# Score tiles of the second batch inside the first softmax chain of a cross-covariance attention and highway kernel, with five copies moved to ScalarE

## Chip, cores, metric

One core of a Trainium2 chip. The time is device microseconds (us) of a whole execution, the median of several; executions of the kernel before agree within about 0.3% here. A ratio is the mean time of one kernel's runs over that of the other's of the same rounds, so it is not quite the ratio of the medians quoted.

## The reference, cut

```python
# q, k, v: (B=4, N=6336, C=256), float32; tau = 1
qn = q / (norm(q, axis=1, keepdims=True) + 1e-6)
kn = k / (norm(k, axis=1, keepdims=True) + 1e-6)
s = kn.transpose(0, 2, 1) @ qn / tau            # (B, C, C): the scores
a = exp(s - s.max(-1)); a /= a.sum(-1) + 1e-9
x = (v @ a).reshape(B * N, C)
H = maximum(x @ w_h, 0); T = sigmoid(x @ w_t + b_t)
out = T * H + (1 - T) * x
```

The scores of a batch need all its rows of q and k; only then can its softmax be taken, and only then the first of its outputs.

## The kernel before

The loads of q and k come in groups of 3 to 8 tiles (a "k group" below). TensorE sums the scores of a batch over 49 tiles of 128 rows and a rest of 64: per tile `S` (k times q, two products of 256 columns) and the squares for the norms in `G` (four products of 128 columns, or two where ScalarE takes the squares of q). A **chain** turns them into matrices: norms, inverse, scaling, exponential, transposition, products with the weights, scaled copies. The outputs come in 100 **slots** of two tiles each: the gate product into a `zbank`, products `h` and `x`, and the transposition of a later pair of v tiles. The score tiles of batches 1 to 3 are mixed into the slots of the batch ahead. Only the first chain has no slots to lie beside; there TensorE multiplied zeros to keep its clock up: with them the granted clock was 1.00 from 37.1 to 45.2, and in a_old_loads, where TensorE stood idle from about 38.0 to 41.0, it fell to 0.50. All instructions stand in the order that the program writes them.

```python
    WARM = (14, 9)             # zero products in the two gaps of the first chain
    CHAIN0 = (0, 0, 0, 4)      # score tiles of batch 1 at four places of it
    PE_BIAS = (8, 67, 75, 97)  # slots whose gate gets its bias by two products; elsewhere ScalarE copies it
# ... at the start of the third group of batch 0:
            load_v(0)
            load_w()
            load_q(QFIRST[1])
            load_k(QFIRST[1])
            load_v(1)
# ... the first chain:
    c0["norms"]()
    c0["invs"]()
    keep_warm(WARM[0])
    fill(CHAIN0[0])
    c0["cq"]()
    c0["logits"]()
    turns = [(t, transpose(t)) for t in range(2)]
    fill(CHAIN0[1])
    keep_warm(WARM[1])
    c0["exps"]()
    c0["at"]()
    fill(CHAIN0[2])
    c0["at_copy"]()
    c0["softmax"]()
    vt_copy(*turns[0])
    c0["first_ahats"]()        # products with the weights, then scaled copies into mr
    vt_copy(*turns[1])
    fill(CHAIN0[3])
    for t in range(2, LOOK):   # LOOK = 3: pair 2
        vt_copy(t, transpose(t))
# ... in first_ahats, its end:
            ah = hx_tile("ah0_0")
            for ic in range(2):
                ahat_half(ah, 0, ic, False)
            for ic in range(2):
                scaled_copy(ah, 0, ic, ic == 0)      # half 0 by ScalarE, half 1 by VectorE
# ... one slot t (cut):
        for s in zs:
            mains(s, zbank[s % 2], 2, True)
            gate_act(s, zbank[s % 2])
        for s in by_pe[:1]:
            vt_copy(s, transpose(s))                 # pair t + 3
        for s in zs:
            seed(s, zbank[s % 2])
        mains(t, h, 1, False)
        mains(t, x, 0, False)
```

All transposed pairs pass through one PSUM bank, `vt_bank`, in two halves by turns.

Of the kernel before, what the change touches and what calls it, by code (L numbers as in the profile page):

```python
# [19 lines left out]
def kernel(  # L20
# [19 lines left out]
    nc = tc.nc  # L40
# [10 lines left out]
    def spans(*sizes):  # L51
        got, s0 = [], 0
        for ns in sizes:
            got.append((s0, ns))
            s0 += ns
        assert s0 == NS
        return got

    QG = [spans(8, 8, 8, 8, 8, 6, 3), spans(4, 8, 8, 8, 8, 8, 5)]
    QG += [spans(5, 8, 8, 8, 8, 8, 4)] * (B - 2)  # L60
    QALL = [(b, g) for b in range(B) for g in range(len(QG[b]))]
    QFIRST = [QALL.index((b, 0)) for b in range(B)]
    QTILES = 8
    QRING = 4
    ORING = 8
    DEFER = 6
    DRAIN = [59, 67, 64, 92, 72, 82]
    VG = [spans(6, 10, 12, 12, 9)] + [spans(12, 12, 12, 13)] * (B - 1)
    VTILES = 13
    VALL = [(b, g) for b in range(B) for g in range(len(VG[b]))]  # L70
# [1 line left out]
    VRING = 4  # L72
    NPAIR = (NS + 1) // 2
    LOOK = 3
    RAMP = 15
    REM_SLOT = 2
    START_US = 1

    WARM = (14, 9)

    CHAIN0 = (0, 0, 0, 4)
    HEAD = sum(CHAIN0)
    P1_END = [18, 42, 63]

    GATES = {14: 2, 19: 2, 20: 0, 22: 0, 25: 2, 27: 2, 33: 0, 54: 2, 55: 1, 60: 2, 66: 0, 68: 0, 70: 0, 95: 2}
    TURNS = {46: 2, 47: 2, 55: 2, 65: 0, 67: 0, 79: 0, 93: 2}
    VTS = 9
    OLAST = 2
    TTS = 6

    TGROUPS = ((26, 6, 73), (38, 6, 79))

    PE_BIAS = (8, 67, 75, 97)

    DVE_SUBS = (98, 99)

# [2 lines left out]



    SQ_RUNS = {1: (5, 20, 30), 2: (8, 18, 26, 35), 3: (10, 21, 34)}
    SQ_TILES = 8
    SQ_CUTS = 4
    SQ_RATE = 2
    LULL = [2, 3, 0, 5]

    EARLY = {"sums": (0, "pre"), "norms": (0, "pre"), "invs": (1, "pre"), "cq": (1, "pe"), "logits": (2, "pre"), "exps": (2, "post"), "softmax": (5, "pre"), "at": (5, "pe"), "at_copy": (6, "pre"), "ahat": (6, "pe"), "ahat_copy": (7, "pre")}
    MID = {"sums": (0, "pre"), "norms": (0, "pre"), "invs": (2, "pre"), "cq": (2, "pe"), "logits": (2, "post"), "exps": (3, "post"), "softmax": (3, "post"), "at": (5, "pe"), "at_copy": (6, "pre"), "ahat": (6, "pe"), "ahat_copy": (7, "pre")}
    LAST = {"sums": (0, "pre"), "norms": (0, "pre"), "invs": (1, "pre"), "cq": (2, "pe"), "logits": (2, "post"), "exps": (3, "pre"), "softmax": (7, "pre"), "at": (8, "pe"), "at_copy": (9, "pre"), "ahat": (9, "pe"), "ahat_copy": (10, "pre")}  # L110
    PLACES = [None, EARLY, MID, LAST]

    ctx.enter_context(tc.manual_schedule())
# [7 lines left out]
    def rows(src2d):  # L121
        return src2d[0:NF, :].rearrange("(p s) c -> p s c", s=NS)
# [4 lines left out]
    def load_q(n):  # L127
        b, g = QALL[n]
        s0, ns = QG[b][g]
        q_t[n] = stream_pool.tile([P, QTILES, C], f16, tag="q_in", bufs=QRING, name=f"q{n}")  # L130
        nc.gpsimd.dma_start(out=q_t[n][:, 0:ns, :], in_=rows(q[b])[:, s0 : s0 + ns, :])  # L131

    def load_k(n):
        b, g = QALL[n]
        s0, ns = QG[b][g]
        k_t[n] = stream_pool.tile([P, QTILES, C], f16, tag="k_in", bufs=QRING, name=f"k{n}")
        nc.gpsimd.dma_start(out=k_t[n][:, 0:ns, :], in_=rows(k[b])[:, s0 : s0 + ns, :])

    def load_v(m):
        b, g = VALL[m]  # L140
        s0, ns = VG[b][g]
        v_t[m] = stream_pool.tile([P, VTILES, C], f16, tag="v_in", bufs=VRING, name=f"v{m}")
        nc.gpsimd.dma_start(out=v_t[m][:, 0:ns, :], in_=rows(v[b])[:, s0 : s0 + ns, :])
# [99 lines left out]
    def squared(b, j):  # L243

        for n, j0 in enumerate(SQ_RUNS.get(b, ())):
            count = SQ_TILES - (n > 0)
# [10 lines left out]
    def squares(b, j):  # L257
# [24 lines left out]
        add_up(len(cuts))  # L282
        more = n < len(SQ_RUNS[b]) - 1
        if more:
# [12 lines left out]
    def add_up(k):  # L297
        while k > 0 and cuts:
            dst, source = cuts.pop(0)
            nc.vector.tensor_reduce(  # L300
                out=dst, in_=source, op=AluOp.add, axis=mybir.AxisListType.XY
            )
            k -= 1
# [225 lines left out]
    def v_of(b, s):  # L529
        if s == NS:  # L530
            return rem_t["v"][:, b, :]
        g = max(i for i in range(len(VG[b])) if VG[b][i][0] <= s)
        return v_t[VFIRST[b] + g][:, s - VG[b][g][0], :]
# [4 lines left out]
    def dma_transposes(t):  # L538

        for n, (s0, ns, at) in enumerate(TGROUPS):  # L540
            if at != t:
# [16 lines left out]

    for s0, ns, _ in TGROUPS:
        for i in range(s0 // 2, (s0 + ns) // 2):  # L560
            BY_DMA[(B - 1) * NPAIR + i] = True

    def nrows(i):
        return [P, REM] if i == NPAIR - 1 else [P, P]

    def transpose(t, bank=None):

        b, i = divmod(t, NPAIR)
        ps = (bank or vt_bank)[:, t % 2]
        nr = nrows(i)  # L570
        for u in range(2):
            vt = v_of(b, 2 * i + u)
            for c in range(2):
                nc.tensor.transpose(  # L574
                    ps[:, u, c, 0 : nr[u]], vt[0 : nr[u], bass.ts(c, P)],
                    ident[0 : nr[u], 0 : nr[u]],
                )
        return ps

    def vt_copy(t, ps):  # L580
        i = t % NPAIR
        sb = work_pool.tile([P, 2, 2, P], f16, tag="vTs", bufs=VTS, name=f"vts{t}")
        if i == NPAIR - 1:
            for u, r in enumerate(nrows(i)):
                nc.vector.tensor_copy(out=sb[:, u, :, 0:r], in_=ps[:, u, :, 0:r])
        else:
            nc.vector.tensor_copy(out=sb, in_=ps)  # L587
        vT_t[t] = sb

    def mains(t, dst, part, seeded):  # L590
        b, i = divmod(t, NPAIR)
        mr = mr_t[b]
        if t in PE_BIAS and seeded:
            for u in range(2):
# [62 lines left out]
    def seed(s, z):  # L657
        if s + 2 < NSLOT and s + 2 not in PE_BIAS:
            nc.scalar.copy(out=z, in_=btb)  # L659
# [34 lines left out]
    def nominal_slot(n):  # L694

        if n < HEAD:
            return -1
        lo, base = RAMP, HEAD
        for i, e in enumerate(P1_END):
            if n < (i + 1) * (NS + 1):  # L700
                return lo + (n - base) * (e - lo) // ((i + 1) * (NS + 1) - base)
            lo, base = e + len(LULL) - 1, (i + 1) * (NS + 1)

    want = []
    for n in range(QFIRST[1] + 1, len(QALL)):
        b, g = QALL[n]
        at = nominal_slot((b - 1) * (NS + 1) + QG[b][g][0])
        for fn, key in ((load_q, "q"), (load_k, "k")):
            want.append((at, len(want), fn, n, ("q", n - QRING), QG[b][g][1]))
    for m in range(2, len(VALL)):  # L710
        b, g = VALL[m]
        at = b * NPAIR + VG[b][g][0] // 2 - LOOK - 1
        dep = ("v", m - VRING) if m >= VRING else None
        want.append((at, len(want), load_v, m, dep, VG[b][g][1]))
    for name in ("q", "k"):
        want.append((REM_SLOT, len(want), load_rem, name, None, 4))
    want.sort()
# [2 lines left out]

    LANES = 8
    TILE_US = 0.305
    SLACK = 3
    landing = [0.0] * LANES
    landed = {}
    dma_at = [0.0]
# [10 lines left out]
    def next_loads(k, now):  # L737
        while k and want and landing[-LANES] <= now + SLACK:
            for i, (_, _, fn, arg, dep, tiles) in enumerate(want[:5]):
# [64 lines left out]
    for j in range(NS):  # L804
        p1_tile(0, j)
        if j == QG[0][1][0]:
            for n in range(QRING, QFIRST[1]):
                load_q(n)
                load_k(n)
            p1_tile(0, NS)  # L810
            seed_banks()
            bias_rows()
            preload_table(Act.Sqrt)
        if j == QG[0][2][0]:
            load_v(0)
            load_w()
            load_q(QFIRST[1])
            load_k(QFIRST[1])
            load_v(1)
    ready = set(used)  # L820
    for key, tiles in (
        ((load_v, 0), VG[0][0][1]), (None, 2), (None, 2), ((load_q, QFIRST[1]), QG[1][0][1]),
        ((load_k, QFIRST[1]), QG[1][0][1]), ((load_v, 1), VG[0][1][1]),
    ):
        note_load(key, tiles, 0.0)

    now = START_US
    done1 = 0
# [14 lines left out]
    def fill(n):  # L843
        nonlocal done1
        for _ in range(n):
            p1_tile(1, done1)
            done1 += 1
# [4 lines that stand above are left out]
    fill(CHAIN0[0])  # L852
    c0["cq"]()
    c0["logits"]()
    turns = [(t, transpose(t)) for t in range(2)]
    fill(CHAIN0[1])
    keep_warm(WARM[1])
    c0["exps"]()
    c0["at"]()
    fill(CHAIN0[2])  # L860
    c0["at_copy"]()
    c0["softmax"]()
    vt_copy(*turns[0])
    c0["first_ahats"]()
    vt_copy(*turns[1])
    fill(CHAIN0[3])
    for t in range(2, LOOK):
        vt_copy(t, transpose(t))
# [13 lines left out]
    for t in range(NSLOT):  # L882
# [3 lines left out]
        run(t, "pre")  # L886
        zs = range(zdone, min(NSLOT, zdone + GATES.get(t, 1)))
        zdone = zs.stop
        turned = range(tdone, min(NSLOT, tdone + TURNS.get(t, 1)))
        tdone = turned.stop  # L890
# [18 lines left out]
        pending.append((t, *products(t, h, x)))  # L909
        add_up(2 if len(cuts) > SQ_RATE else 1)  # L910
        run(t, "post")
# [16 lines left out]
        if pb < len(P1_END):  # L928
            left = P1_END[pb] - t
            if 0 <= t - end1 < len(LULL):  # L930
                due = LULL[t - end1]
            else:
# [18 lines left out]
        if t not in (end1 - 1, end1):  # L951
            next_loads(2, now)
        room = DEFER - sum(t >= at for at in DRAIN)
        out_now = 0
# [42 lines left out]
```

## Time and profile before

| | before |
|---|---|
| median of 3 runs | 274.08 us (274.0 to 274.6) |
| span of the profiled run | 272.1 us |
| TensorE busy | 252.7 us, 93% |
| scores of batch 0 end / chain ends / last score tile / last product | 37.1 / 45.2 / 207 / 265.2 us |

The prediction shows the lines. Read from the outside in: the page's shares and chain first, then windows cut at the stages, then the order of time inside the stage that the change touches. Two lines that it did not show matter later. The first is of the list of TensorE's waits from 37 us on (who waits, for whom; us in total, times, longest); in the order of time this one wait stands at 218.59, in the last chain. The second is the transposition of pair 3, just ahead of the first h:

```profile
PE vt_bank L574 <- DVE vts L587: 0.3, 1, 0.3
...
46.08 0.38 PE L574 MATMUL vt_bank<-ident,v 128*128 128x128 f16 x4
```

### The profile page before, as it was taken

The numbers are of one execution on the slowest core, as the hardware profiler recorded it, in microseconds if no ns is written. First come the engines' busy times: TensorE is split into PE (matmuls) and PEld (weight loads), VectorE is DVE, ScalarE is ACT, GpSimd is POOL, SyncE is SP. The second block draws the span as 40 slices with busy tenths as digits, with TensorE's granted clock in tenths as the row PEclk, the third lists the DMA queues.
The fourth block names the chain that finished last, engine by engine and source line by source line (L and its number), as shares of the span: only waits on it lengthen the run. The fifth ranks groups of instructions, "written<-read, shape, count | busy, mean of one in ns | idle before, by whom it ended". The sixth has DMA issues, their size and how long they took to land.

```text
span 272.1 us, 6836 instructions
## 1 busy us (share of the span) xinstructions
PE 252.7 (93%) x2735; PEld 224.0 (82%) x2735; DVE 203.4 (75%) x438; ACT 164.5 (60%) x296; POOL 171.5 (63%) x191
## 2 busy tenths in 40 slices
PE   0599898999999999999999999999999999999990
PEld 0588786999999987999999988799998887999870
DVE  1600036996678877699999867798889999999983
ACT  1040046767474497787584489576764976778850
POOL 7014351897665298565876784754655986889970
PEclk9999999999999999999999999999999999999998
DMA  6999999999999999999999999999999799998583
GB/s 120 214 213 213 210 209 211 213 213 214 215 210 217 212 182 214 212 281 255 246 281 288 263 243 288 215 255 257 287 271 361 219 302 301 319 348 340 211 332 107
DMA packets 19862, 66.44 MB, mean 244 GB/s; under 512 B 4979, under 2 KB 7286, under 8 KB 16886
## 3 DMA queue, kind: packets, MB, share of 16 engines
q0 software_dynamic: 11744, 39.13, 73.0%
q1 hardware_dynamic: 8006, 26.81, 26.1%
q8 instruction: 21, 0.34, 0.5%
q10 hardware_dynamic: 80, 0.07, 0.1%
q14 instruction: 11, 0.09, 0.1%
HBM read 78.38 MB, written 25.95 MB: 383 GB/s over the span
## 4 chain that ended last, share of the span: by engine, by line
PE 82%; DMA 8%; DVE 5%; issue 2%; ACT 1%; POOL 0%; DVEq 0%; ACTq 0%; POOLq 0%
PE zbank L601 15%; PE h L601 15%; PE x L601 15%; PE S L227 15%; DMA k<-in_k_dram 8%; PE vt_bank L574 7%; PE G L230 7%; PE G L233 4%; DVE th L671 2%; PE ah L466 1%; DVE ux L676 1%; DVE vts L587 1%; DVE at_sb L332 1%; ACT tt L655 0%; POOL q L131 0%
## 5 line engine op out<-in xcount | busy, mean ns | idle before, releaser
L686 POOL TENSOR_TENSOR o<-th,ux 128x512 f32<-128x512 f32 x95 | 120.9, 1277 | 53.2 <-DVE ux L676 46.4
L601 PEld LDWEIGHTS <-vts 128*128 128x128 f16 x1128 | 103.7, 98 | 13.9 <-issue 3.8
L227 PE MATMUL S<-q,k 128*128 128x256 f16 x392 | 82.1, 277 | 11.1 <-DMA k<-in_k_dram 11.1
L655 ACT ACTIVATE tt<-zbank 128x512 f32<-128x512 f32 x100 | 58.9, 596 | 53.2 <-PE zbank L601 49.5
L230 PE MATMUL G<-k 128*128 128x128 f16 x392 | 73.8, 222 | 0.0
L671 DVE SCALAR_TENSOR_TENSOR th<-h,tt 128x512 f32<-128x512 f32 (+1 forms) x104 | 68.8, 665 | 6.1 <-ACT tt L655 1.0
L676 DVE SCALAR_TENSOR_TENSOR ux<-tt,x 128x512 f32<-128x512 f32 (+1 forms) x104 | 67.8, 655 | 0.0
L601 PE MATMUL x<-mr,vts 128*128 128x256 f16 (+1 forms) x376 | 56.9, 273 | 0.1
L601 PE MATMUL h<-mr,vts 128*128 128x256 f16 (+1 forms) x376 | 56.9, 273 | 0.0
L659 ACT COPY zbank<-btb 128x512 f32<-128x512 f32 x94 | 55.0, 590 | 2.6
L601 PE MATMUL zbank<-mr,vts 128*128 128x256 f16 (+1 forms) x376 | 55.9, 273 | 0.0
L587 DVE COPY vts<-vt_bank 128x512 f16<-128x512 f16 x90 | 37.7, 419 | 22.2 <-PE vt_bank L574 21.3
L227 PEld LDWEIGHTS <-k 128*128 128x128 f16 x392 | 38.9, 99 | 15.6 <-DMA k<-in_k_dram 11.6
L230 PEld LDWEIGHTS <-k 128*128 128x128 f16 x392 | 38.9, 99 | 0.7
L574 PE MATMUL vt_bank<-ident,v 128*128 128x128 f16 x368 | 35.8, 219 | 0.3 <-DVE vts L587 0.3
L233 PE MATMUL G<-q 128*128 128x128 f16 x246 | 34.5, 223 | 0.0
L574 PEld LDWEIGHTS <-v 128*128 128x128 f16 x368 | 28.0, 98 | 3.4 <-issue 1.3
L131 POOL DMA_DIRECT2D q<-in_q_dram x28 | 15.9, 568 | 21.6 <-PE G L233 16.1
L275 ACT ACTIVATE sq<-q 128x512 f32<-128x512 f16 (+1 forms) x46 | 24.2, 569 | 0.0
L332 DVE SCALAR_TENSOR_TENSOR at_sb<-G,ident 128x128 f16<-128x128 f32 x16 | 3.7, 287 | 25.9 <-PE G L233 25.8
L233 PEld LDWEIGHTS <-q 128*128 128x128 f16 x246 | 19.4, 100 | 1.7
L300 DVE TENSOR_REDUCE sq<-sq 128x64 f32<-128x512 f32 x28 | 18.2, 675 | 0.0
(104 smaller groups left out, 148.5 us busy)
## 6 DMA issues: line engine op xcount, KB each, us to landing
out_dram<-o SPq DMA_DIRECT2D x23, 1024.0 KB, 9.5
q<-in_q_dram POOLq DMA_DIRECT2D x20, 512.0 KB, 13.0
k<-in_k_dram POOLq DMA_DIRECT2D x20, 512.0 KB, 15.1
v<-in_v_dram POOLq DMA_DIRECT2D x11, 768.0 KB, 16.0
v<-in_v_dram POOLq DMA_DIRECT2D x3, 832.0 KB, 20.9
out_dram<-o SPq DMA_DIRECT2D x4, 256.0 KB, 2.0
q<-in_q_dram POOLq DMA_DIRECT2D x3, 320.0 KB, 9.9
k<-in_k_dram POOLq DMA_DIRECT2D x3, 320.0 KB, 10.9
```

The costliest lines, as they stand in the source:

```text
L227: nc.tensor.matmul(S[:, c, :], kc, qq[0:nr, :], start=first and c == 0, stop=last and c == 1)
L230: nc.tensor.matmul(G[:, c, :], kc, kc, start=first and c == 0, stop=False)
L233: nc.tensor.matmul(G[:, 2 + c, :], qc, qc, start=False, stop=last and c == 1)
L275: nc.scalar.activation(out=sq[:, o // 2, :, u : u + src.shape[1]].rearrange("p c u -> p u c"), in_=src, func=Act.Square,)
L574: nc.tensor.transpose(ps[:, u, c, 0 : nr[u]], vt[0 : nr[u], bass.ts(c, P)], ident[0 : nr[u], 0 : nr[u]],)
L587: nc.vector.tensor_copy(out=sb, in_=ps)
L601: nc.tensor.matmul(dst[0:r, u, :], vT_t[t][:, u, kt, 0:r], mr[:, part, kt, :], start=(not seeded and kt == 0 and (u == 0 or i == NPAIR - 1 ...
L655: nc.scalar.activation(out=tt_t[s], in_=z, func=Act.Sigmoid)
L659: nc.scalar.copy(out=z, in_=btb)
L671: nc.vector.scalar_tensor_tensor(out=th[pr, us, :], in0=h[pr, us, :], scalar=0.0, in1=tt[pr, us, :], op0=AluOp.max, op1=AluOp.mult,)
L676: nc.vector.scalar_tensor_tensor(out=ux[pr, us, :], in0=tt[pr, us, :], scalar=1.0, in1=x[pr, us, :], op0=AluOp.subtract, op1=AluOp.mult,)
L686: last = eng.tensor_tensor(out=ot[pr, o0 + us.start : o0 + us.stop, :], in0=th[pr, us, :], in1=ux[pr, us, :], op=AluOp.subtract,)
```

## The change

Intent: give TensorE real work in the two gaps of the first chain, so that the four score tiles no longer stand between the chain and the first slot. They need q and k of batch 1 earlier, so these loads go ahead of v and the weights. The copies of the first two transposed pairs move up in VectorE's order; five later ones go to ScalarE; two bias pairs less on TensorE; the lists that place later work are retuned.

```diff
-    DEFER = 6
+    DEFER = 7
-    WARM = (14, 9)
-    CHAIN0 = (0, 0, 0, 4)
+    WARM = (6, 2)
+    CHAIN0 = (2, 2, 0, 0)
+    ACT_COPIES = (16, 41, 46, 60, 82)
-    PE_BIAS = (8, 67, 75, 97)
+    PE_BIAS = (3, 97)
-    SQ_RUNS = {1: (5, 20, 30), 2: (8, 18, 26, 35), 3: (10, 21, 34)}
+    SQ_RUNS = {1: (9, 20), 2: (5, 13, 23, 31), 3: (9, 18, 26, 33)}
 ... (GATES, TURNS, TGROUPS, DRAIN, SQ_RATE, LULL, PLACES, load constants: cut)
     vt_copy:
+        copy = nc.scalar.copy if t in ACT_COPIES else nc.vector.tensor_copy
         if j == QG[0][2][0]:
+            load_q(QFIRST[1])
+            load_k(QFIRST[1])
             load_v(0)
             load_w()
-            load_q(QFIRST[1])
-            load_k(QFIRST[1])
             load_v(1)
     c0["logits"]()
+    fill(CHAIN0[1])
     turns = [(t, transpose(t)) for t in range(2)]
-    fill(CHAIN0[1])
     keep_warm(WARM[1])
     c0["exps"]()
+    vt_copy(*turns[0])
     c0["at"]()
     fill(CHAIN0[2])
     c0["at_copy"]()
+    vt_copy(*turns[1])
     c0["softmax"]()
-    vt_copy(*turns[0])
     c0["first_ahats"]()
-    vt_copy(*turns[1])
```

More of the change, by code (lines that the diff above doesn't have):

```diff
@@ L65 @@
     ORING = 8
-    DEFER = 6
-    DRAIN = [59, 67, 64, 92, 72, 82]
+    DEFER = 7
+    DRAIN = [62, 61, 58, 84, 68, 79]
     VG = [spans(6, 10, 12, 12, 9)] + [spans(12, 12, 12, 13)] * (B - 1)
@@ L74 @@
     LOOK = 3
-    RAMP = 15
-    REM_SLOT = 2
-    START_US = 1
-    WARM = (14, 9)
-    CHAIN0 = (0, 0, 0, 4)
+    RAMP = 13
+    REM_SLOT = 1
+    START_US = 0
+    WARM = (6, 2)
+    CHAIN0 = (2, 2, 0, 0)
     HEAD = sum(CHAIN0)
     P1_END = [18, 42, 63]
-    GATES = {14: 2, 19: 2, 20: 0, 22: 0, 25: 2, 27: 2, 33: 0, 54: 2, 55: 1, 60: 2, 66: 0, 68: 0, 70: 0, 95: 2}
-    TURNS = {46: 2, 47: 2, 55: 2, 65: 0, 67: 0, 79: 0, 93: 2}
+    GATES = {13: 2, 14: 2, 20: 0, 24: 0, 25: 2, 28: 2, 36: 0, 51: 2, 54: 1, 55: 1, 61: 2, 68: 0, 69: 0, 72: 0, 95: 2}
+    TURNS = {50: 2, 67: 0, 93: 2}
     VTS = 9
@@ L89 @@
     TTS = 6
-    TGROUPS = ((26, 6, 73), (38, 6, 79))
-    PE_BIAS = (8, 67, 75, 97)
+    TGROUPS = ((26, 6, 70), (38, 6, 84))
+    ACT_COPIES = (16, 41, 46, 60, 82)
+    PE_BIAS = (3, 97)
     DVE_SUBS = (98, 99)
     V_HELD = {}
-    SQ_RUNS = {1: (5, 20, 30), 2: (8, 18, 26, 35), 3: (10, 21, 34)}
+    SQ_RUNS = {1: (9, 20), 2: (5, 13, 23, 31), 3: (9, 18, 26, 33)}
     SQ_TILES = 8
     SQ_CUTS = 4
-    SQ_RATE = 2
-    LULL = [2, 3, 0, 5]
-    EARLY = {"sums": (0, "pre"), "norms": (0, "pre"), "invs": (1, "pre"), "cq": (1, "pe"), "logits": (2, "pre"), "exps": (2, "post"), "softmax": (5, "pre"), "at": (5, "pe"), "at_copy": (6, "pre"), "ahat": (6, "pe"), "ahat_copy": (7, "pre")}
-    MID = {"sums": (0, "pre"), "norms": (0, "pre"), "invs": (2, "pre"), "cq": (2, "pe"), "logits": (2, "post"), "exps": (3, "post"), "softmax": (3, "post"), "at": (5, "pe"), "at_copy": (6, "pre"), "ahat": (6, "pe"), "ahat_copy": (7, "pre")}
-    LAST = {"sums": (0, "pre"), "norms": (0, "pre"), "invs": (1, "pre"), "cq": (2, "pe"), "logits": (2, "post"), "exps": (3, "pre"), "softmax": (7, "pre"), "at": (8, "pe"), "at_copy": (9, "pre"), "ahat": (9, "pe"), "ahat_copy": (10, "pre")}
+    SQ_RATE = 4
+    LULL = [2, 3, 0, 7]
+    EARLY = {"sums": (0, "pre"), "norms": (0, "pre"), "invs": (1, "pre"), "cq": (1, "pe"), "logits": (2, "pre"), "exps": (2, "post"), "softmax": (4, "pre"), "at": (5, "pe"), "at_copy": (6, "pre"), "ahat": (6, "pe"), "ahat_copy": (7, "pre")}
+    MID = {"sums": (0, "pre"), "norms": (0, "pre"), "invs": (2, "pre"), "cq": (2, "pe"), "logits": (2, "post"), "exps": (3, "post"), "softmax": (3, "post"), "at": (4, "pe"), "at_copy": (5, "pre"), "ahat": (5, "pe"), "ahat_copy": (6, "pre")}
+    LAST = {"sums": (0, "pre"), "norms": (0, "pre"), "invs": (1, "pre"), "cq": (3, "pe"), "logits": (3, "post"), "exps": (5, "pre"), "softmax": (8, "pre"), "at": (9, "pe"), "at_copy": (9, "post"), "ahat": (10, "pe"), "ahat_copy": (11, "pre")}
     PLACES = [None, EARLY, MID, LAST]
@@ L582, in vt_copy @@
         sb = work_pool.tile([P, 2, 2, P], f16, tag="vTs", bufs=VTS, name=f"vts{t}")
+        copy = nc.scalar.copy if t in ACT_COPIES else nc.vector.tensor_copy
         if i == NPAIR - 1:
             for u, r in enumerate(nrows(i)):
-                nc.vector.tensor_copy(out=sb[:, u, :, 0:r], in_=ps[:, u, :, 0:r])
+                copy(out=sb[:, u, :, 0:r], in_=ps[:, u, :, 0:r])
         else:
-            nc.vector.tensor_copy(out=sb, in_=ps)
+            copy(out=sb, in_=ps)
         vT_t[t] = sb
@@ L722 @@
     TILE_US = 0.305
-    SLACK = 3
+    SLACK = 2
     landing = [0.0] * LANES
@@ L821 @@
     for key, tiles in (
-        ((load_v, 0), VG[0][0][1]), (None, 2), (None, 2), ((load_q, QFIRST[1]), QG[1][0][1]),
-        ((load_k, QFIRST[1]), QG[1][0][1]), ((load_v, 1), VG[0][1][1]),
+        ((load_q, QFIRST[1]), QG[1][0][1]), ((load_k, QFIRST[1]), QG[1][0][1]),
+        ((load_v, 0), VG[0][0][1]), (None, 2), (None, 2), ((load_v, 1), VG[0][1][1]),
     ):
```

## The prediction

> **What bounds the kernel now.** I read the head of the page first (busy shares, slices, chain), then a table of windows that I cut at the stages, then the order of time of the first chain.
>
> ```profile
> PE 252.7 (93%) x2735; PEld 224.0 (82%) x2735; DVE 203.4 (75%) x438; ACT 164.5 (60%) x296; POOL 171.5 (63%) x191
> ...
> DMA  6999999999999999999999999999999799998583
> GB/s 120 214 213 213 210 209 211 213 213 214 215 210 217 212 182 214 212 281 255 246 281 288 263 243 288 215 255 257 287 271 361 219 302 301 319 348 340 211 332 107
> ...
> PE 82%; DMA 8%; DVE 5%; issue 2%; ACT 1%; POOL 0%; DVEq 0%; ACTq 0%; POOLq 0%
> ```
>
> TensorE carries 82% of the chain that ended last, and the DMA part (8%) is the wait for the first loads of batch 0. But the DMA row stands at 9 for nearly the whole span, at a flat 213 GB/s for the first 17 slices: the loads come at a fixed rate, so a faster TensorE can run into them. The windows are: scores of batch 0 end at 37.1; the first chain (norms, exponential, transposition, products with the weights) lasts until 45.2; then come 100 slots of outputs, into which the scores of batches 1 to 3 are mixed until 207; then outputs alone.
>
> ```profile
> core 0: us, PE busy (x) PEld busy (x) DVE busy (x) ACT busy (x) POOL busy (x), PEclk, DMA share, GB/s
> 37.10:45.20 8.10, 7.17 (x76) 5.86 (x75) 5.89 (x26) 5.97 (x13) 2.83 (x5) 1.00 1.19 213
> 45.20:60.00 14.80, 14.72 (x157) 13.27 (x155) 13.73 (x27) 10.10 (x17) 11.54 (x14) 1.00 1.05 213
> 60.00:91.90 31.90, 31.90 (x379) 29.45 (x376) 22.98 (x41) 18.13 (x34) 18.90 (x21) 1.00 1.07 214
> 91.90:150.60 58.70, 58.70 (x647) 52.56 (x644) 51.11 (x105) 42.84 (x80) 42.46 (x47) 1.00 1.04 243
> 150.60:207.00 56.40, 56.40 (x631) 50.55 (x630) 46.07 (x96) 39.03 (x71) 34.39 (x36) 1.00 1.05 265
> 207.00:220.00 13.00, 12.60 (x122) 10.72 (x121) 12.56 (x34) 10.78 (x20) 10.74 (x11) 1.00 0.86 257
> 220.00:265.20 45.20, 45.20 (x441) 38.59 (x438) 43.52 (x84) 33.10 (x57) 37.47 (x31) 1.00 0.91 315
> ```
>
> After 45.2 TensorE has no gap to win except about 1 us in 207 to 220. From 207 on VectorE is nearly full too (12.56 of 13.00, 43.52 of 45.20), so there it is a second bound. TensorE's 7.17 busy in the first chain is partly false work: the products of zeros.
>
> ```profile
> 37.19 1.69 PE L838 MATMUL warm<-zeros 128*128 128x256 f16 x14
> ...
> 38.98 0.71 PE L391 MATMUL cq<-dcat,taus 128*128 128x128 f32 x4
> ...
> 39.97 1.15 PE L838 MATMUL warm<-zeros 128*128 128x256 f16 x9
> ...
> 41.23 0.29 PE L456 MATMUL at<-ident,e 128*128 128x128 f16 x2
> ...
> 42.53 1.05 PE L466 MATMUL ah<-wht,at_sb 128*128 128x256 f16 x8 [0.52 <-DVE at_sb L462]
> ...
> 44.12 0.48 DVE L491 TENSOR_SCALAR mr<-ah,rinv 128x256 f16<-128x256 f32 x1 [0.15 <-ACT mr L489]
> ...
> 46.30 0.60 PE L601 MATMUL h<-mr,vts 128*128 128x256 f16 x4
> ```
>
> To be seen: two runs of zero products fill waits for VectorE and ScalarE. The last scaled copy of the matrix ends at 44.12 + 0.48 = 44.60, but the first h starts only at 46.30, because the four score tiles of batch 1 stand between (in the same order of time their S products start at 43.41, 43.85, 44.29 and 44.74, and the next transposition at 45.18).
>
> [...] 14 zero products take 1.69 us with the tail of the last (0.27), 1.42/13 = 0.109 each; a score tile, two products of 256 columns and four of 128, starts every 0.44 us. [...] The granted clock here is 1.00 in every window of the chain[...]. [...] GpSimd sat 16.1 us in three waits before loads of q for TensorE's last use of a buffer.
>
> **The change part by part.**
>
> *Four tiles into the chain.* 14 zeros (1.53 us at 0.109) become 6 zeros and two tiles: 0.65 + 0.87 = 1.52. The second run, 9 zeros with 8 transpositions (0.98 + 0.44), becomes two tiles, 8 transpositions and 2 zeros: 0.87 + 0.44 + 0.22 = 1.53 against 1.42. It has room: the zeros ended about 0.35 before the exponential's transposition at 41.23. So 15 zero products (1.64 us) are replaced by tiles that then no longer stand at 43.41 to 45.18. Does the chain then let h start that much earlier? h needs the last scaled copy, at 44.60. The two copies of transposed v (0.42 each on VectorE) now stand ahead of the at copy and of the reciprocal. I place them: the first from 41.66 to 42.08 (the at copy was at 42.05: +0.03), the second to 42.84, the reciprocal to 43.0, the first scaled copy at 43.03 instead of 42.96. The last copy waits for ScalarE's, which is not moved. So h at about 44.7 instead of 46.3: **-1.6 us**.
>
> *Loads.* In the order before, v and weights were issued from 25.56 and q, k of batch 1 at 30.00 and 31.58. They landed at 37.28 (v), 38.69 (second weight), 39.92 (q) and 41.14 (k). In front of v they need the buffers of the fourth group, whose last product is at 28.0, so issue at about 28.3 and 28.8. The queue is full then (the last k of batch 0 lands at 35.47), so they follow it: 4 + 4 tiles at 0.31 us a tile (16 tiles per 4.9 us in the first groups) give q 36.7 and k 37.9. Six zeros end at 37.8. v follows at 39.8, for transpositions at about 40.4; weights at 41.1, for use at 42.53. All just fit: a 0.1 to 0.2 us wait for k, hidden before the cq product at 38.98.
>
> *Bias by products.* Slots 8, 67, 75, 97 become 3, 97: 4 products fewer, 4 x 0.109 = **-0.44 us** of TensorE; two copies more on ScalarE (590 ns each), which is 73% busy in 220 to 265.
>
> *Five copies to ScalarE.* VectorE loses 5 x 0.42, ScalarE gains 5 of about 0.59 (the 128x512 ScalarE copy out of PSUM in the chain took 0.59). Mostly beside TensorE; I give it nothing, except that only one (slot 82) lies in the last stage.
>
> *Slots shifted.* The instruction order shows the same number of transpositions, gates and score tiles, but two transpositions more after the last score tile: 0.44 us of TensorE and two VectorE copies move from before 207 to after it. The last chain's steps are spread over three more slots, which should save some of the 1 us of gaps there. I count **-0.3 us** for both.
>
> *The load limit.* From landings and first uses of each k group (two S weight loads a tile), the smallest margins in the mixed stages are 1.34 us (issued 69.36, landed 81.22, used 82.56) and 1.40 (landed 165.5, used 166.9); the others are over 2.3. A TensorE 1.6 us earlier takes up the first: **+0.3 us**. The second is helped by one more store held back (stores wait seven deep, not six).
>
> Sum: -1.6 - 0.44 - 0.3 + 0.3 = -2.04 us, so 274.08 becomes 272.0.
>
> **The rivals.** (1) The tiles wait for k in the chain. If q and k landed near 39 and not 37.9, cq, and the whole chain, would slip by about 1 us: 273.0. For it: the issue now waits for buffer and GpSimd's order, and v and weights slip too. Against: the queue holds 8 us of loads when they are issued. (2) Loads bound the mixed stage: every tile early is waited back, so the 1.6 is cut to the 1.34 margin or less, and the second margin takes more: 272.8 to 273.5. For it: DMA at 9 everywhere; against: most margins exceed 2.3. (3) VectorE bounds the last stage: two copies more there and one away, [...] the bias gain (slots 67 and 75 are both there) is not felt: 272.6. For it: 43.52 of 45.20 busy. (4) The retimed later chain and gates close all its 1 us of gaps as well: 271.0.
>
> **Range and chances.** The centre is the sum; rivals 1 to 3 cost up to 1.5 us together, rival 4 gains 1. Range 270.6 to 273.5. 2% is 5.5 us, more than twice anything found removable, so within 2% has 0.96.
>
> **What would show each step.** Products of zeros x8 and bias products x4; first h near 44.7; q and k of batch 1 landing before 38; TensorE's last products near 263 instead of 265.2; scores of batch 3 ended near 205. It would be wrong if the order of time shows a DMA wait before an S product in the chain or near 81, or if the windows after the last score tile grow by over 0.5 us.

## The result, and the profile after

The changed kernel took 272.97 us (median of 4, 272.74 to 273.24) against 274.12 for the kernel before in the same rounds; ratio 0.9955, interval 0.9938 to 0.9972. In a second set of rounds (run a_again) it took 272.75 against 274.25, ratio 0.9948. The gain of 1.1 to 1.5 us is inside the stated range but well short of the 2.04 of the sum.

The head of the page after: busy shares, DMA slices, chain that ended last.

```profile
PE 250.3 (92%) x2716; PEld 221.8 (82%) x2716; DVE 200.6 (74%) x433; ACT 167.0 (62%) x300; POOL 171.6 (63%) x191
...
DMA  6999999999999999999999999999999989999465
...
PE 83%; DMA 8%; DVE 4%; issue 1%; ACT 1%; POOL 0%; DVEq 0%; ACTq 0%; POOLq 0%
```

TensorE has 19 products fewer, as counted: 15 of zeros and 4 of bias. It still carries the chain, and no load took its place. The windows after, cut at the same events (columns as in the prediction):

```profile
37.30:44.40 7.10, 6.12 (x68) 4.88 (x66) 5.43 (x26) 5.97 (x13) 1.21 (x3) 1.00 1.23 207
44.40:60.00 15.60, 14.85 (x156) 13.54 (x156) 14.96 (x30) 10.62 (x18) 12.37 (x15) 1.00 1.05 213
...
205.80:220.00 14.20, 13.88 (x140) 11.96 (x138) 13.83 (x35) 11.81 (x21) 11.80 (x11) 1.00 1.01 346
220.00:264.10 44.10, 43.90 (x426) 37.19 (x424) 42.40 (x84) 33.06 (x57) 36.41 (x30) 1.00 0.85 286
```

The row to stop at is the second. Before, TensorE was busy 14.72 of 14.80 in the window after the chain; now it is idle for 0.75 us there, and VectorE is busy 14.96 of 15.60. The order of time after, for the chain:

```profile
37.34 0.82 PE L841 MATMUL warm<-zeros 128*128 128x256 f16 x6
...
38.53 0.22 PE L232 MATMUL G<-k 128*128 128x128 f16 x1 [0.25 <-DVE at_sb L334]
...
39.30 0.66 PE L393 MATMUL cq<-dcat,taus 128*128 128x128 f32 x4
...
41.50 0.28 PE L458 MATMUL at<-ident,e 128*128 128x128 f16 x2
...
42.80 1.05 PE L468 MATMUL ah<-wht,at_sb 128*128 128x256 f16 x8 [0.52 <-DVE at_sb L464]
...
44.39 0.48 DVE L493 TENSOR_SCALAR mr<-ah,rinv 128x256 f16<-128x256 f32 x1
...
44.79 0.41 DVE L590 COPY vts<-vt_bank 128x512 f16<-128x512 f16 x1
...
45.26 0.38 PE L576 MATMUL vt_bank<-ident,v 128*128 128x128 f16 x4 [0.76 <-DVE vts L590]
...
45.48 0.60 PE L604 MATMUL h<-mr,vts 128*128 128x256 f16 x4
```

The tiles fit, and with them in place of 15 zeros the granted clock stayed at 1.00 from 37.3 to 44.4, but not for nothing. k of batch 1 landed at 37.72 and was first used at 37.89. At 38.53 a product into `G` waits 0.25 us until VectorE has read batch 0's norms out of it, and this holds the chain's product cq, which stands behind the tiles: cq came 1.96 us after the first zero, against 1.79 in the kernel before, and the product of at 4.16 against 4.04, so the chain is 0.12 us later. And the first h came at 45.48, not at 44.7. Between the last scaled copy and h there are now two steps one after the other: VectorE's copy of pair 2, and TensorE's transposition of pair 3, which waits 0.76 us for that copy though it writes the other half of `vt_bank` (two banks were not tried). In TensorE's list of waits this line grew from one wait to two, the 0.76 and, at 215.91, the 0.3 of the kernel before; the wait for `G` is new:

```profile
PE vt_bank L576 <- DVE vts L590: 1.1, 2, 0.8
PE ah L468 <- DVE at_sb L464: 0.5, 1, 0.5
PE G L232 <- DVE at_sb L334: 0.2, 1, 0.2
```

**A ruler without the jitter of the first loads.** The scores of batch 0 wait for loads, and these jitter: in the traces the first zero product, which follows the last of these scores at once, starts anywhere from 37.19 to 37.75. (The third k group landed within 19.09 and 19.34 in the first six traces, the fourth between 24.53 and 25.09, and the first zero came 12.66 us after the fourth in every trace; why the fourth varies stays open.) So I count from that product. The table gives the start of the first h of slots 0 and 1, the start of the product that follows the last score tile of batch 3, and the modelled end of TensorE's last product, all in us after the first zero product, read from the traces.

| kernel | first zero at | h, slot 0 | h, slot 1 | scores of batch 3 done | last product ends |
|---|---|---|---|---|---|
| before | 37.19 | 9.11 | 10.64 | 169.99 | 228.09 |
| after | 37.34 | 8.14 | 9.67 | 168.57 | 226.79 |
| a_again | 37.34 | 8.14 | 9.67 | 168.56 | 226.78 |
| a_zeros | 37.75 | 9.22 | 10.75 | 169.65 | 227.86 |
| b_head | 37.64 | 8.14 | 9.67 | 169.01 | 227.11 |
| a_turn_late | 37.61 | 7.06 | 10.07 | 168.96 | 227.19 |
| a_turn_late2 | 37.32 | 7.06 | 9.46 | 168.36 | 226.93 |
| a_copy_early | 37.32 | 7.52 | 9.11 | 168.05 | 226.27 |
| a_old_bias | 37.45 | 8.14 | 9.67 | 168.56 | 227.14 |
| a_dve_copies | 37.32 | 8.13 | 9.67 | 168.56 | 227.01 |
| a_old_loads | 37.22 | 12.15 | 13.69 | 172.58 | 230.80 |
| a_early_bias97 | 37.44 | 7.52 | 9.11 | 167.78 | 226.00 |
| a_early_bias0 | 37.60 | 7.65 | 9.18 | 167.85 | 225.99 |

From the last product to the end of the span it is 6.82 to 6.84 us in every trace, so nothing hides in the tail. Two runs of the changed kernel agree within 0.01 on this ruler, and for the ten other runs below the timed ratios (times 274.2 us) give the same differences to a_again within 0.1 us, but for a_old_loads (3.6 for 4.0) and a_early_bias0 (-1.0 for -0.8). It does not take out everything: each row is one trace, and a single slow instruction in it counts in full. Three rows have one (a_zeros, a_dve_copies, a_turn_late2, below). On it the change gains 228.09 - 226.79 = 1.30 us: 0.97 by slot 1, another 0.45 by the end of the scores (1.42 in all there), and 0.12 given back after them.

### The profile page after: what moved, and what is told of

Its sections match the earlier page's. It is cut to its first block, busy times and chain, and to the rows that moved or that the text cites. A ratio compares the mean times of both kernels' runs of the same rounds, so it can differ in the third digit from the quotient of the medians. Undisturbed runs are those within 1.5% of the kernel's fastest.

```text
span 271.0 us, 6790 instructions
## 1 busy us (share of the span) xinstructions
PE 250.3 (92%) x2716; PEld 221.8 (82%) x2716; DVE 200.6 (74%) x433; ACT 167.0 (62%) x300; POOL 171.6 (63%) x191
## 4 chain that ended last, share of the span: by engine, by line
PE 83%; DMA 8%; DVE 4%; issue 1%; ACT 1%; POOL 0%; DVEq 0%; ACTq 0%; POOLq 0%
PE zbank L604 16%; PE h L604 15%; PE x L604 15%; PE S L229 15%; DMA k<-in_k_dram 8%; PE vt_bank L576 7%; PE G L232 7%; PE G L235 4%; PE ah L468 1%; DVE th L674 1%; DVE ux L679 1%; PE sums L324 1%; DVE vts L590 1%; PE cq L398 0%; ACT tt L658 0%
## 5 line engine op out<-in xcount | busy, mean ns | idle before, releaser
L662 ACT COPY zbank<-btb 128x512 f32<-128x512 f32 x96 | 56.3, 592 | 2.6
L590 DVE COPY vts<-vt_bank 128x512 f16<-128x512 f16 x85 | 35.6, 419 | 19.3 <-PE vt_bank L576 19.0
```

The lines of the kernel that those rows point to most:

```text
L590: copy(out=sb, in_=ps)
L662: nc.scalar.copy(out=z, in_=btb)
```

## The experiments

Eleven runs, all correct. Theory after reading the trace: the tiles in the chain are worth 0.8 to 1.0 us, and the rest of the 1.6 was lost to the new wait between TensorE and VectorE. Rivals: the load rate takes the gain back; VectorE's own work bounds these slots; the gain is from the retuned lists. (Those lists were tested only together, in b_head and a_zeros.)

**a_again.** The changed kernel unchanged.

> The changed kernel once more, as the mark for the other runs of this chip. Expected: 0.4% under the kernel before (about -1.15 us), first h at 45.5 us, 0.8 us ahead of the kernel before. If the scores of batch 0 end 0.16 us later than in the kernel before only because loads jitter, that difference should change here.

272.75 us (272.71 to 273.33) against 274.25; ratio 0.9948 (0.9936 to 0.9961). The first zero came at 37.34 again, so this repeat did not show the jitter; other kernels did.

**a_zeros.**

```diff
-    WARM = (6, 2)
-    CHAIN0 = (2, 2, 0, 0)
+    WARM = (14, 9)
+    CHAIN0 = (0, 0, 0, 4)
```

> The changed kernel with the four tiles put back after the chain and 14 and 9 zero products in their place; everything else stays changed. Theory (the tiles in the chain bring 0.8 us and the retuned lists 0.3 to 0.4): first h at about 46.4, time about 273.8, 0.8 us over the changed kernel. Rival (the retuned lists bring the gain, the moved tiles nothing): time as the changed kernel, 273.0. Rival as predicted (tiles worth 1.6): 274.6.

274.16 us (273.66 to 274.37), ratio 0.9990 (0.9977 to 1.0002): nearly all the gain is gone. On the ruler the last product ends 1.07 us later than in the changed kernel, and 1.08 stands at slot 1 already. So the tiles' place is worth about 1 us, not 1.6 and not zero, and it is kept to the end. Of the 1.08, 0.11 is not the tiles' doing: one short VectorE step of the chain (L362, from 38.80) took 0.28 us in this trace and 0.17 in the kernel before, cq came at 1.90 instead of 1.79, and at at 4.15 instead of 4.04. Without it 0.97 is left, the same as in b_head. (The median is 1.4 us above that of a_again; by the ratios it is 1.15.)

**b_head.** The kernel before with the first part of the change alone.

```diff
 (on the kernel before: WARM, CHAIN0, load order and copy order as in the change; nothing else)
```

> The kernel before with the first part of the change alone: load order, tiles in the chain, the order of the copies; none of the retuned lists, copies by ScalarE or bias slots. Theory (head worth 0.8, handed on to the end): first h at 45.5 and 273.3 us. Rival (the load rate takes it back in the mixed stages, margin of 1.34 us before the k group issued near 69): first h at 45.5, but TensorE waits for DMA near 81 or 165, and the end gains under 0.3 us.

273.27 us, ratio 0.9961 (0.9948 to 0.9973). On the ruler -0.97 at slot 1 and -0.98 at the last product, against the kernel before. TensorE waited for no load after the chain. The rival of the load rate falls: the gain made in the chain arrives whole. The tight k group kept its room, 1.27 us for 1.34: GpSimd issues it behind the subtraction of a slot, and as the slots came earlier, so did this (67.06 instead of 67.58), the issue (68.84 instead of 69.36) and the landing (80.77 instead of 81.22). All other parts of the change together are worth the rest: 227.11 - 226.79 = 0.32 us.

**a_turn_late.** The transposition of pair 3 behind x in slot 0, its copy behind the products of slot 0.

```diff
-        for s in by_pe[:1]:
+        for s in by_pe[:1] if t else []:
             vt_copy(s, transpose(s))
 ...
+        late = [] if t else [(s, transpose(s)) for s in by_pe]
         run(t, "pe")
         pending.append((t, *products(t, h, x)))
+        for s, ps in late:
+            vt_copy(s, ps)
```

> The changed kernel, with the transposition that stands ahead of the first h (pair 3) moved behind the first x, its copy behind the first two products. Theory (the first h is held not by the last scaled copy but by this transposition, which waits for VectorE's copy of pair 2 out of the same PSUM bank): first h at about 44.95 instead of 45.48 and 0.3 to 0.5 us off the total, about 272.5. Rival (h is held by the last scaled copy or by VectorE's backlog): first h moves by under 0.1 and the total stays at 273.0.

273.28 us, ratio 0.9962 (0.9948 to 0.9975): slower than the changed kernel. The order of time says what happened:

```profile
45.20 0.49 PE L604 MATMUL h<-mr,vts 128*128 128x256 f16 x3 [0.25 <-DVE mr L493]
45.52 0.60 PE L604 MATMUL x<-mr,vts 128*128 128x256 f16 x4
...
47.46 0.38 PE L576 MATMUL vt_bank<-ident,v 128*128 128x128 f16 x4 [0.68 <-DVE vts L590]
```

h did start 1.08 us earlier on the ruler (7.06), with one product; its other three waited for the scaled copy itself, until 7.59. But one slot later pair 4's transposition waits 0.68 for the copy of pair 3, which stands behind two products on VectorE. The wait moved on; slot 1 is 0.40 late. So the diagnosis of the first h was right and the cure wrong.

**a_turn_late2.** As that, with the copy ahead of the products of slot 0.

```diff
-        for s in by_pe[:1]:
+        for s in by_pe[:1] if t else []:
             vt_copy(s, transpose(s))
 ...
-        for s in by_pe[1:]:
+        for s in by_pe[1:] if t else by_pe:
             vt_copy(s, transpose(s))
```

> As the last run, but the copy of pair 3 stays ahead of the first two products on VectorE, so that only TensorE's order is changed in slot 0. Counted from the first zero product of the chain (37.34 in the changed kernel), h of slot 1 came 9.68 us later there and 10.07 in the last run. Theory (TensorE and VectorE wait for each other by way of the bank of transposed v; the last run only moved the wait one slot on, behind the products): h of slot 1 after about 9.3, and 0.2 to 0.4 us less in all. Rival (VectorE's own work bounds these slots): h of slot 1 after 9.6 or more and no gain.

273.06 us (272.73 to 273.26), ratio 0.9954: no gain. On the ruler slot 1 is 0.21 earlier, half of what the theory said, and the scores end 0.21 earlier; then the last chain takes 0.35 back, and the last product ends 0.14 later than in the changed kernel. In that stretch TensorE's x products wait for VectorE's th (0.2 us at 215.10), which they don't do in the changed kernel. The whole 0.35 enters at one place: at 212.56 VectorE's th starts 0.71 us after the copy ahead of it, in a_again 0.36 after (212.08, 212.44), though its h had ended at 212.08. What held it the trace does not show, so it is not shown that the edit costs this.

**a_copy_early.** Pair 2's transposition and copy ahead of the last scaled copies. VectorE was idle there for 0.13 us in the changed kernel (44.26 to 44.39), ahead of its last scaled copy; in the kernel before it was 0.15 us, put down by the list to ScalarE's scaled copy out of the same `ah`.

```diff
             for ic in range(2):
                 ahat_half(ah, 0, ic, False)
+            between()              # vt_copy(2, transpose(2)), taken from behind first_ahats
             for ic in range(2):
                 scaled_copy(ah, 0, ic, ic == 0)
```

> The changed kernel with pair 2's copy out of the transposition bank put ahead of VectorE's last scaled copy, which waits 0.13 us for ScalarE anyway. Theory: the transposition of pair 3 comes 0.5 us sooner, the last scaled copy 0.25 us later, first h about 0.3 us earlier, 0.3 us less in all. Rival (VectorE's work bounds): no gain.

272.49 us (272.18 to 272.54), ratio 0.9931 (0.9918 to 0.9943): the fastest so far.

```profile
44.15 0.42 DVE L591 COPY vts<-vt_bank 128x512 f16<-128x512 f16 x1
44.48 0.48 DVE L493 TENSOR_SCALAR mr<-ah,rinv 128x256 f16<-128x256 f32 x1
...
44.62 0.38 PE L577 MATMUL vt_bank<-ident,v 128*128 128x128 f16 x4
44.84 0.66 PE L605 MATMUL h<-mr,vts 128*128 128x256 f16 x4
```

With the same work on every engine, the copy now stands ahead of the scaled copy, the transposition and h go 0.62 earlier than in the changed kernel, and slot 1 is 0.56 early; 0.52 of it arrives at the last product. (The rest is lost between slots 46 and 47, by the look of it to a load: a k group of batch 3 landed at 164.23 and was used at 164.27.) The rival that VectorE's work bounds these slots falls: only the order of two of its instructions changed. The expected 0.3 was too low, since the last scaled copy slipped by only 0.1.

**a_old_bias.**

```diff
-    PE_BIAS = (3, 97)
+    PE_BIAS = (3, 67, 75, 97)
```

> The changed kernel with the bias of slots 67 and 75 by products again (the kernel before had slots 8, 67, 75, 97). By the prediction's sum: four products more, +0.44 us, all in the last stage. Rival 3 (VectorE bounds the last stage, so TensorE's products there cost nothing): under 0.15 us.

273.15 us, ratio 0.9959 (0.9945 to 0.9973). Identical on the ruler up to the end of the scores, then 0.35 later at the last product. So TensorE's products do count in the last stage, for 80% of the 0.44 that the sum put there. Rival 3 falls as stated.

**a_dve_copies.**

```diff
-    ACT_COPIES = (16, 41, 46, 60, 82)
+    ACT_COPIES = ()
```

> The changed kernel with the five copies back on VectorE. As predicted (they lie beside TensorE): under 0.2 us more. Rival (VectorE is the second bound [...]): up to 0.7 us more, from slot 41 on.

273.20 us, ratio 0.9959 (0.9946 to 0.9971). On the ruler TensorE's h stands where it stood up to slot 92, within 0.01 us; then it is 0.22 to 0.23 late, to the end. So four of the copies are worth nothing, and the copy of slot 82 had been absorbed ten slots earlier, though a copy by ScalarE took 580 ns in the changed kernel and one by VectorE 418. The 0.23 enters at one product of VectorE, here in the changed kernel and in this run:

```profile
251.88 0.69 DVE L674 SCALAR_TENSOR_TENSOR th<-h,tt 128x512 f32<-128x512 f32 x1
...
252.21 0.69 DVE L674 SCALAR_TENSOR_TENSOR th<-h,tt 128x512 f32<-128x512 f32 x1 [0.40 <-PE x L604]
```

The gate that it needs ended at 251.80 there and 251.77 here, and x, which the list names, it does not read. So it started 0.33 us late for a reason that the trace does not show; whether the copies bring it about is not shown either (the intervals of the two ratios overlap).

**a_old_loads.** The changed kernel with v and weights loaded ahead of q and k again.

```diff
-            load_q(QFIRST[1])
-            load_k(QFIRST[1])
             load_v(0)
             load_w()
+            load_q(QFIRST[1])
+            load_k(QFIRST[1])
             load_v(1)
```

> The changed kernel with the loads in the old order (v and weights ahead of q and k of batch 1), the tiles still inside the chain. In the kernel before, k of batch 1 landed 3.95 us after the first zero product (41.14 against 37.19). Theory: the first tile can't start before that; TensorE holds the chain's own product behind it, so cq comes at about 4.9 instead of 1.96 us after the first zero, and the total is about 2.9 us over the changed kernel, some 275.7. Rival (the loads' order is a detail, the tiles find room anyway): under 0.5 us more.

276.68 us (275.71 to 276.96), ratio 1.0079 (1.0058 to 1.0100), 4.0 us over the changed kernel on the ruler instead of 2.9. The first lines are of the order of time, the rest of windows (PE, PEld, DVE, ACT, POOL, granted clock):

```profile
41.01 0.39 PE L229 MATMUL S<-q,k 128*128 128x256 f16 x1 [2.98 <-DMA k<-in_k_dram]
41.30 0.42 PE L229 MATMUL S<-q,k 128*128 128x256 f16 x1
```

```profile
38.00:41.00 3.00, 0.03 (x1) 0.00 (x0) 1.41 (x10) 1.85 (x4) 1.15 (x3) 0.90 1.15 222
41.00:43.00 2.00, 1.99 (x13) 1.74 (x14) 0.00 (x0) 0.00 (x0) 0.00 (x0) 0.50 1.01 193
43.00:45.00 2.00, 2.00 (x24) 1.87 (x23) 0.75 (x2) 0.59 (x3) 0.00 (x0) 0.80 1.36 206
```

The tile waits 2.98 us for k, and the chain's product, which the program writes behind it, starts only at 42.69, 5.47 us after the first zero (1.96 in the changed kernel). And the clock falls to 0.50: in windows of 0.2 us it was 1.00 up to 40.2, 0.95 in 40.2 to 40.4 and 0.50 from 40.4, 2.4 us after TensorE fell idle at about 38.0. The matmul of 256 columns takes 0.42 instead of 0.27 us, from 41.0 until about 43.8 (0.27 again at 43.89). That is the part that I had not expected. One of the four runs had a mean clock of 0.996 and took 275.71, what the theory said; the others had 0.984 to 0.990 and took 276.65 to 276.96. The loads' order is not a detail of the change but its condition; it worked with 0.17 us to spare in the changed kernel (k landed at 37.72, first used at 37.89). A little less is forgiven: in a_copy_early k landed at 38.25 and was used at 38.29, and the product of at still stood 4.16 after the first zero.

**a_early_bias97** and **a_early_bias0.** On a_copy_early, the remaining bias products removed.

```diff
-    PE_BIAS = (3, 97)
+    PE_BIAS = (97,)        # a_early_bias97
+    PE_BIAS = ()           # a_early_bias0
```

> The better version of the last runs (pair 2's copy ahead of the last scaled copy), with the bias of slot 3 by ScalarE's copy as well. If TensorE bounds the first slots: 2 products fewer, 0.2 us less, 272.3. If ScalarE's copy and gate chain is as near to the bound there: no gain or a small loss.

272.06 us (271.94 to 272.26), ratio 0.9919 (0.9906 to 0.9933). On the ruler -0.22 against a_copy_early from slot 3 on, the price of the two products, and -0.27 at the last product, as the 0.05 that a_copy_early lost before slot 47 is not lost here (the same k group landed at 161.56, used at 164.08).

> The last version with the bias of slot 97 by ScalarE's copy too, so no bias products at all. If TensorE still bounds the end: 0.2 us less, about 271.85. If the tail hangs on ScalarE's copy and gate (the gate of slot 97 comes in a tail without other work): no gain or a loss of a few tenths.

271.96 us (271.77 to 272.21), ratio 0.9910 (0.9894 to 0.9927), against a_early_bias97 no difference that the runs resolve. In its trace the transposition of pair 3 waits 0.25 us for the second v load at 45.02, and h comes 0.13 late on the ruler. That is a load's jitter: this load landed 7.37 us after the first zero here and 7.20 and 6.65 after it in the other two kernels with the early copy. From slot 96 on 0.09 is won back, where the bias of slot 97 was. Both beat both kernels of the case.

## Why the prediction was right or wrong

The range held, and the centre was 1.0 us too low. By its terms:

- **Four tiles into the chain, -1.6 us: mechanism right, size wrong; this is the step that failed.** Measured -0.97 (b_head; a_zeros says the same when its slow step is taken off). "So h at about 44.7 instead of 46.3" let h follow the last scaled copy by 0.1 us; that is h at 7.51 on the ruler, and it came at 8.14. Of the missing 0.63, 0.51 is the path behind that copy: h followed it by 0.61 (44.87 to 45.48). The prediction overlooked that in TensorE's order pair 3's transposition stands ahead of h, that it needs VectorE's copy of pair 2, and that this copy stood behind the scaled copies. a_copy_early shows the cause: with the copy moved up, slot 0's h comes 0.62 earlier (7.52 against 8.14). The other 0.12 is the chain itself, whose last scaled copy ended at 7.53 instead of 7.41: the tiles waited for `G`, which the prediction did not see, where it expected a short and hidden wait for k. The order of time before held a hint: the gate's four products from 45.40, 0.109 apart, leave TensorE free for the transposition of pair 3 at about 45.84, but it starts at 46.08, just after the copy of pair 2 (45.60 and 0.42). By this estimate it already waited 0.24 us, behind the four tiles that the change takes away.
- **Loads in the chain: right.** q was put at 36.7 and landed at 36.47, k at 37.9 and landed at 37.72, v at 39.8 (39.59), weights at 41.1 (40.93). That the issue waits for the buffer in GpSimd's order was right too (28.73, put at 28.3). a_old_loads shows rival 1 in a stronger form (k at 40.97, not 39).
- **Bias, -0.44: nearly right.** Measured 0.35 for the two slots (a_old_bias).
- **Slots shifted, -0.3: failed.** The two transpositions that moved past the scores gained 0.44 ahead of them, as counted: 169.99 - 168.57 = 1.42, which is 0.97 + 0.45 (no run tests this move alone). After the scores they were paid back: the last stage grew by 0.12 although two bias pairs (0.35) and one VectorE copy left it: two transpositions and two copies came in, and TensorE's idle time in the last two windows before its end is 0.52 us after (14.20 - 13.88 and 44.10 - 43.90) against 0.40 before. The spreading of the chain's steps showed no gain; the diff makes it end one slot later, not three as the prediction says.
- **Load limit, +0.3: did not come.** The prediction let TensorE come earlier and the loads stay. They come with it, as GpSimd issues them among its work for the slots: in b_head, with the old lists, the tightest k group kept a margin of 1.27 us for 1.34. In the changed kernel it landed at 80.76 and was first used at 82.86, a margin of 2.10. Here the use did not move earlier, because ScalarE now squares 15 tiles of q in batch 1 instead of 22 (the diff's SQ_RUNS), which leaves TensorE seven tiles' squares more before that point, by an estimate 14 x 0.055 = 0.8 us (two such products at 43.74 in the kernel before, the next product at 43.85). (The total of squares is the same; they moved.)
- **Copies by ScalarE, 0: right as far as a_dve_copies shows.** Its 0.23 comes from one late product, with no link to a copy shown.
- **Rival 4** (all gaps of the last chain closed) is not seen. 2% was out of reach, as said.

Of the sum's -2.04, the ruler has -1.30. The medians of the two sets of rounds gave 1.15 and 1.50, on either side of it.

## What to carry to other kernels

When work that stands between two stages is moved into a gap, what it used to hide can come out (here a wait of 0.76 us): follow every instruction that stands ahead of the next one in its engine's order, not only the operand it needs. Where two engines hand one buffer back and forth, the order of two short instructions on the second engine was worth about half as much as the work moved (0.52 us for 0.97, with no work taken away), and shifting the wait on the first engine alone only moved it one step on (0.76 us at slot 0 became 0.68 one slot later in a_turn_late). Count short differences from an event behind the jitter of the first loads; then 0.1 us can be read from single traces (two of the changed kernel agree within 0.01 us here), if you also look up where the difference enters. Twice here it was one VectorE product that started 0.3 us late, far from the edit.
